# State-space scan and two MLP layers: the norm of a whole block of four units at once, state and outputs of a unit in one PSUM bank, first scores in other banks

## The chip, the cores and the metric

The kernel runs on one core of a Trainium2 chip. The metric is the time of one execution in device microseconds (us). A core has TensorE (PE: matmuls into PSUM; PEld are its weight loads), VectorE (DVE), ScalarE (ACT), GpSimd (POOL) and SyncE (SP, whose queue issues nearly all DMAs here). PSUM has eight banks of 512 fp32 columns on 128 partitions.

## What is computed

Three stages in a row, on 3072 tokens of 256 features. A state-space scan in chunks, over 4 batches and 8 heads:

```python
cum = np.cumsum(la, axis=-1)                      # la: log of the decays of a chunk
L = np.exp(cum[:, :, :, None] - cum[:, :, None, :]) * causal
CB = np.einsum('bhin,bhjn->bhij', Cc, Bc)
y_intra = np.einsum('bhij,bhjd->bhid', CB * L, xc)
y_inter = np.einsum('bhin,bhnd->bhid', Cc, state) * decay_to_i[:, :, :, None]
state = decay_full[:, :, None, None] * state + np.sum(Bx, axis=2)
```

Then a gated MLP behind a norm over the features, and a second MLP:

```python
rms = np.sqrt(np.mean(x * x, axis=-1, keepdims=True) + 1e-06)
xn = x / rms * rms_g
g = xn @ w_gate
x = (g / (1 + np.exp(-g))) * (xn @ w_val) @ w_out     # 256 -> 1536 -> 256
h = x @ w_in                                          # 256 -> 2048
out = (np.maximum(h, 0) + np.log1p(np.exp(-np.abs(h)))) @ w_out2
```

## The kernel before, in words

**Units and blocks.** The scan works on units: 128 tokens of one batch, all eight heads. There are 24, four batches by six; unit u is batch u % 4. Four units (one of each batch) make a block of 512 tokens, on which the MLP layers run; there are six blocks. Features lie on the partitions, two halves of 128 (`KD` = 2).

**One unit** (`unit`). DVE makes the products of decays by two scans of 128x512 (`ab`); the factors come from DRAM (`a_clip`) or, for the first four units, are copied across partitions by PE (`spread` of the decays, `p<-Sm,ident`). PE makes scores C·B into two PSUM tiles (`gps`); units 0 to 7 from tiles `hw`, later ones from `st` and `cz`. DVE multiplies each with the products (`decay`, 128x512). PE then runs the unit's groups: the outputs `yp` from state and chunk, and the new state's sum `sp`, in separate PSUM tiles. DVE updates the state `S` of the batch from `sp` (line 584; for the first four units ACT copies it); POOL builds the masked state `Sm` for the next unit of that batch.

**The norm of one unit** follows it (lines 589 to 621). ACT squares `yp` (`sq`, line 595); PE sums the squares over the features by matmuls with one column (`msum`, `a<-mean,sq`); DVE takes the inverse root in eight steps of 128x1 (`root`, lines 602 to 607: two to begin with, then three turns of two); PE spreads the root over the partitions (`a<-ident,rs`, one fp32 matmul of 128x128 that the trace shows as two passes); ACT scales `yp` by the gains (line 617); DVE multiplies (line 619), ACT copies the high part (`xxh`) and DVE subtracts for the low part (`xxl`, line 306). High and low parts are what the MLP's three-pass matmuls read.

**The MLP.** For each block, layer one has 12 steps `f` of twelve 128x512 matmuls (`front1`: `wg`, `wv`) and six (`back`: `wo`); layer two 16 steps of six (`front2`: `wi`) and six (`back`: `wp`). Between front and back stand an activation on ACT, a product on DVE in layer one, and the split into high and low part (`hw`, ACT line 299, DVE line 306). The order of stages is layer one of blocks 0 and 1, layer two of 0 and 1, then both layers of 2, 3, 4, 5. Units of later blocks run among the matmuls of the blocks before.

**Weights** come in 34 chunks of 512 KB through three buffers `wr`; ACT and DVE turn a chunk into high and low part. For the first four chunks PE makes the low part (`p<-wr,wil`). Forty matmuls with a constant (`filler`, `p<-mean`) stand in the first 44 us.

**Who sets the order.** A planner (`Plan`) writes it out. Every operation has an engine, an estimated length, a rank and the buffers that it reads and writes; `emit` runs through time with these estimates and takes at each point the operation that can start first, the lower rank ahead. What comes out is one fixed list per engine, in which each engine waits for its operands. The root's eight steps are estimated at 65 ns each. PSUM has three pools: `p` with four banks (fronts, decay spreads, fillers), `a` with two (scores, `yp`, `sp` and the norm's `nb` of units from block 1 on), `t` with two (the backs' sums, and `yp` in block 0). `SCORES_P` = 4 puts the scores of units 0 to 3 into `p`.

```python
DVE(0, rank[0], root, [nb, "mean"], [rs, ss], port=False, ns=8 * 65)
PE(220, rank[0], lambda: mm(nb()[:, 0:P], rs()[:, 0:1].to_broadcast([P, P]), ident, True, True), [rs, "ident"], [nb], 512)
```

Of the kernel before, what the change touches and what calls it, by code (L numbers as in the profile page):

```python
# [17 lines left out]
P = 128  # L18
# [8 lines left out]
NATIVE, SCORES_P, SPREAD = 8, 4, 4  # L27
# [14 lines left out]
XN_REST = ("dve",)  # L42
# [20 lines left out]
class Plan:  # L63
# [48 lines left out]
    def emit(self):  # L112
# [122 lines left out]
def tile_ssd_then_swiglu_then_softplus_mlp(  # L235
# [176 lines left out]
    xnT = {}  # L412

# [22 lines left out]
    def unit(u):  # L436
# [86 lines left out]
        gps = [pbuf("p" if u < SCORES_P else "a", [P, 4 * P]) for _ in range(2)]  # L523
# [28 lines left out]
        yp = pbuf("t" if blk_of[u] == 0 else "a", [P, KD, P])  # L552
# [34 lines left out]
        nxt()  # L587
        sq = buf("sq", [P, KD, P], F32, 2)
        ss, rs = buf("ss", [P, 1], F32, 2), buf("rs", [P, 2], F32, 2)
        nb = pbuf("a", [P, P + 1])  # L590

        def msum():
            for k in range(KD):
                mm(nb()[:, P:P + 1], sq()[:, k], mean, k == 0, k == KD - 1)
        ACT(256, rank[0], lambda: act.activation(out=sq(), in_=yp(), func=ACTF.Square), [yp], [sq])
        PE(400, rank[0], msum, [sq, "mean"], [nb], 8)

        def root():


            y, t = rs()[:, 0:1], rs()[:, 1:2]
            dve.tensor_scalar(out=ss(), in0=nb()[:, P:P + 1], scalar1=1e-6, scalar2=0.5, op0=ALU.add, op1=ALU.mult)  # L602
            dve.tensor_scalar(out=y.bitcast(I32), in0=ss().bitcast(I32), scalar1=-0.5, scalar2=float(0x5F3759DF - 2 ** 22 - 2 ** 31),  # L603
                              op0=ALU.mult, op1=ALU.add)
            for _ in range(3):
                dve.scalar_tensor_tensor(out=t, in0=y, scalar=y, in1=ss(), op0=ALU.mult, op1=ALU.mult)  # L606
                dve.scalar_tensor_tensor(out=y, in0=t, scalar=1.5, in1=y, op0=ALU.subtract, op1=ALU.mult)  # L607
        DVE(0, rank[0], root, [nb, "mean"], [rs, ss], port=False, ns=8 * 65)
        PE(220, rank[0], lambda: mm(nb()[:, 0:P], rs()[:, 0:1].to_broadcast([P, P]), ident, True, True), [rs, "ident"], [nb], 512)
# [41 lines left out]
    def front1(t, f, rank, new_table, early=False):  # L651
# [3 lines left out]
        xk = [(x, o) for x in (xh, xl) for o in range(bl["nu"])]  # L655
# [197 lines left out]
```

## Time and profile before

| | |
|---|---|
| median of 3 runs | 686.77 us (686.3 to 689.27) |
| the profiled execution | 689.41 us |
| its span (first to last instruction) | 686.9 us |
| PE busy | 668.5 us, 97% |
| DVE busy | 363.3 us, 53% |
| ACT busy | 311.6 us, 45% |
| POOL busy | 18.4 us, 3% |

The busy time of an engine is the time in which at least one of its instructions runs. The ends of matmuls are modelled, so that a matmul's listed length reaches into the next one. A wait is the idle time of an engine just before an instruction, put down to whatever released it last.

### The profile page before, as it was taken

The page shows a single profiled execution, that of the slowest core. Times are in us where ns is not written, and L with a number is a line of the kernel's source. Part 1 is how long each engine was busy: PE and PEld are TensorE (multiplying, and loading weights), DVE is VectorE, ACT ScalarE, POOL GpSimd, SP SyncE. Part 2 cuts the span into 40 slices and gives each one's busy share as a digit, 9 for nine tenths or more (in the row PEclk, how much of TensorE's full clock was granted, in tenths as well). Part 3 has the DMA queues.
Part 4 walks back from the last instruction along what each step waited for, and adds up shares of the span by engine and source line. Part 5 has one row for each costly group of instructions (what it writes and reads, how often), then busy time and mean ns, then how long its engine had stood idle before and what let it go on. Part 6 is the DMA issues. An engine that isn't in the chain of part 4 may idle for free.

```text
span 686.9 us, 9171 instructions
## 1 busy us (share of the span) xinstructions
PE 668.5 (97%) x3492; PEld 530.0 (77%) x3492; DVE 363.3 (53%) x722; ACT 311.6 (45%) x553; POOL 18.4 (3%) x28
## 2 busy tenths in 40 slices
PE   8899999999999999999999999999999999999997
PEld 6667778887778887778888777888777888887785
DVE  5989987787662226683433765432574322233222
ACT  4256746775444445232544332544423444422543
POOL 1000000001000000000000000000000000000000
PEclk9999999999999999999999999999999999999999
DMA  7546686657320004310231411050500000000000
GB/s 237 168 162 219 202 280 182 203 172 234 123 80 31 0 1 142 101 66 0 80 119 47 147 53 63 5 189 6 168 25 1 0 1 0 31 0 1 0 1 31
DMA packets 36778, 61.36 MB, mean 89 GB/s; under 512 B 3424, under 2 KB 18304, under 8 KB 36736
## 3 DMA queue, kind: packets, MB, share of 16 engines
q1 hardware_dynamic: 36304, 59.23, 26.8%
q10 hardware_dynamic: 432, 1.57, 0.7%
q8 instruction: 27, 0.44, 0.3%
q14 instruction: 15, 0.12, 0.1%
HBM read 47.58 MB, written 13.21 MB: 88 GB/s over the span
## 4 chain that ended last, share of the span: by engine, by line
PE 87%; DVE 8%; DMA 2%; issue 1%; SPq 1%; ACT 1%; DVEq 0%; ACTq 0%
PE p L268 48%; PE t L268 32%; PE a L268 7%; DVE rs L606 2%; DVE rs L607 2%; DMA xc<-in_xc 1%; DVE s L667 1%; DMA s<-in_ab 1%; DVE rs L603 1%; DVE ss L602 0%; DVE ab L500 0%; DVE hw L306 0%; ACT hw L299 0%; DVE xxl L500 0%; SPq L470 0%
## 5 line engine op out<-in xcount | busy, mean ns | idle before, releaser
L306 DVE TENSOR_TENSOR hw<-s,hw 128x512 fp32r<-128x512 f32 x162 | 111.8, 692 | 185.0 <-ACT hw L299 184.4
L299 ACT ACTIVATE hw<-s 128x512 fp32r<-128x512 f32 x162 | 101.8, 631 | 131.5 <-DVE s L667 103.6
L268 PE MATMUL t<-hw,wph 128*128 128x512 f32 x384 | 121.9, 398 | 0.2 <-DVE hw L306 0.2
L679 ACT ACTIVATE s<-p 128x512 f32<-128x512 f32 x96 | 57.0, 598 | 109.3 <-PE p L268 108.3
L667 DVE TENSOR_TENSOR s<-s,p 128x512 f32<-128x512 f32 x72 | 49.4, 686 | 75.1 <-PE p L268 68.1
L268 PEld LDWEIGHTS t<-hw,wph 128*128 128x128 f32 x384 | 71.2, 188 | 18.3 <-issue 1.0
L268 PE MATMUL t<-hw,woh 128*128 128x512 f32 x264 | 84.6, 401 | 0.3 <-DVE hw L306 0.2
L268 PE MATMUL p<-xxh,wih 128*128 128x512 f32 x192 | 76.3, 397 | 0.0
L268 PE MATMUL t<-hw,wpl 128*128 128x512 f32 x192 | 75.9, 396 | 0.0
L268 PE MATMUL p<-xxh,wil 128*128 128x512 f32 x192 | 75.9, 395 | 0.0
L268 PE MATMUL p<-xxl,wih 128*128 128x512 f32 x192 | 75.6, 394 | 0.2 <-DVE xxl L708 0.2
L663 ACT ACTIVATE s<-p 128x512 f32<-128x512 f32 x72 | 43.0, 598 | 45.3 <-PE p L268 42.8
L268 PE MATMUL p<-xxh,wgh 128*128 128x512 f32 x144 | 58.7, 408 | 0.0
L268 PE MATMUL p<-xxh,wvh 128*128 128x512 f32 x144 | 58.7, 408 | 0.0
L268 PEld LDWEIGHTS t<-hw,woh 128*128 128x128 f32 x264 | 48.1, 188 | 12.2 <-issue 0.8
L268 PE MATMUL p<-xxh,wgl 128*128 128x512 f32 x144 | 57.5, 399 | 0.0
L268 PE MATMUL p<-xxh,wvl 128*128 128x512 f32 x144 | 57.3, 398 | 0.0
L268 PE MATMUL p<-xxl,wgh 128*128 128x512 f32 x144 | 57.1, 396 | 0.0
L268 PE MATMUL p<-xxl,wvh 128*128 128x512 f32 x144 | 57.0, 396 | 0.0
L268 PE MATMUL t<-hw,wol 128*128 128x512 f32 x132 | 52.3, 396 | 0.0
L500 DVE TENSOR_TENSOR_SCAN ab<-ab,ident 128x512 f32<-128x512 f32 x40 | 48.4, 1217 | 0.0
L268 PEld LDWEIGHTS p<-xxl,wih 128*128 128x128 f32 x192 | 36.1, 188 | 9.2 <-DVE xxl L708 0.7
(113 smaller groups left out, 823.8 us busy)
## 6 DMA issues: line engine op xcount, KB each, us to landing
wr<-in_w SPq DMA_DIRECT2D x31, 512.0 KB, 3.3
ab<-a_clip SPq DMA_DIRECT2D x20, 512.0 KB, 4.0
parts<-wr SPq DMA_DIRECT2D x16, 512.0 KB, 3.7
xc<-in_xc SPq DMA_DIRECT2D x20, 256.0 KB, 4.1
st<-parts SPq DMA_DIRECT2D x16, 256.0 KB, 2.8
cz<-parts SPq DMA_DIRECT2D x32, 128.0 KB, 3.1
out_y<-s SPq DMA_DIRECT2D x12, 256.0 KB, 3.3
wr<-in_bc SPq DMA_DIRECT2D x8, 256.0 KB, 3.5
```

The source lines that it names most:

```text
L268: pe.matmul(out=o, lhsT=l, rhs=r, start=start, stop=stop, skip_group_check=True)
L299: ways = {"act": (act_ns(n), lambda: act.activation(out=out(), in_=in_(), func=ACTF.Copy)), "dve": (dve_ns(n, sbuf), lambda: dve.tensor_co ...
L306: return lambda: eng.tensor_tensor(out=out(), in0=in_(), in1=f32(hi()), op=ALU.subtract)
L500: DVE(512, rank[0], lambda t=t, d=d: dve.tensor_tensor_scan(out=t(), data0=d(), data1=ident4, initial=0.0, op0=ALU.mult, op1=ALU.add), dk ...
L603: dve.tensor_scalar(out=y.bitcast(I32), in0=ss().bitcast(I32), scalar1=-0.5, scalar2=float(0x5F3759DF - 2 ** 22 - 2 ** 31), op0=ALU.mult, ...
L606: dve.scalar_tensor_tensor(out=t, in0=y, scalar=y, in1=ss(), op0=ALU.mult, op1=ALU.mult)
L607: dve.scalar_tensor_tensor(out=y, in0=t, scalar=1.5, in1=y, op0=ALU.subtract, op1=ALU.mult)
L663: ACT(n, rank - EPI, lambda: act.activation(out=s()[:, 0:n], in_=ps[0]()[:, 0:n], func=ACTF.Silu), [ps[0]], [s, "table"] if new_table else ...
L667: DVE(n, rank - EPI, lambda: dve.tensor_tensor(out=s()[:, 0:n], in0=s()[:, 0:n], in1=ps[1]()[:, 0:n], op=ALU.mult), [s, ps[1]], [s], port= ...
L679: ACT(n, rank - EPI, lambda: act.activation(out=s()[:, 0:n], in_=hp()[:, 0:n], func=ACTF.Softplus), [hp], [s, "table"] if new_table and f ...
```

## The change

The norm leaves `unit` and becomes a function `norm` of several units: all four of a block at once, for block 0 of the first three and then of the fourth (`NORMS`). A unit now only squares and scales its outputs, into tiles of the whole block (`ysq`: squares under the tag `xxh`, scaled outputs under `xxl`, for which the xx pools' order is set by `rank`). When the last unit of a part is done, PE sums the squares of all its units one after the other, DVE takes the roots of up to four columns together, PE spreads them into one bank of up to 512 columns, and DVE multiplies, ACT copies and DVE subtracts over 384 or 512 columns at a time. For more than one unit the root has eleven steps, since the step with a scalar per partition becomes two plain multiplies. The planner's estimate for a step is 185 ns instead of 65.

`yp` and `sp` become two parts of one PSUM tile `ys` (256 and 64 columns). Only the first matmul into it clears the bank. All its readers name the one tile, so that the update of the state by DVE, the square and the scalings by ACT are kept from reading the bank at the same time. Scores of all units go into pool `a` (`SCORES_P` is gone), the sums and spreads of block 0 into pool `p`.

```diff
-NATIVE, SCORES_P, SPREAD = 8, 4, 4
+NATIVE, SPREAD = 8, 4
+NORMS = {0: [3, 1]}
...
-            l.sort(key=lambda b: (ops[b.ops[0]][1], b.ops[0]))
+            l.sort(key=lambda b: (ops[b.ops[0]][1] if b.rank is None else b.rank, b.ops[0]))
...
-        gps = [pbuf("p" if u < SCORES_P else "a", [P, 4 * P]) for _ in range(2)]
+        gps = [pbuf("a", [P, 4 * P]) for _ in range(2)]
...
-        yp = pbuf("t" if blk_of[u] == 0 else "a", [P, KD, P])
+        ys = pbuf("t" if blk_of[u] == 0 else "a", [P, KD * P + 2 * HD])
+        yp = lambda: ys()[:, 0:KD * P].rearrange("p (k i) -> p k i", k=KD)
+        sp = lambda: ys()[:, KD * P:KD * P + 2 * HD]
...
-        sp = None if last else pbuf("a", [P, 2 * HD])
...
-                    mm(sp()[32 * r:32 * r + 32], br()[:, 32 * r:32 * r + 32], xr()[:, 2 * HD * r:2 * HD * (r + 1)], True, True)
+                    mm(sp()[32 * r:32 * r + 32], br()[:, 32 * r:32 * r + 32], xr()[:, 2 * HD * r:2 * HD * (r + 1)], first, False)
...
-                    in1=sp(), op0=ALU.mult, op1=ALU.add), [S[b], sp, (xbt, "p")], [S[b]])
+                    in1=sp(), op0=ALU.mult, op1=ALU.add), [S[b], ys, (xbt, "p")], [S[b]])
...
+        ACT(256, rank[0], lambda: act.activation(out=sq()[:, :, c], in_=yp(), func=ACTF.Square), [ys], [(sq, o)])
+        for k in range(KD):
+            ACT(128, rank[0], lambda k=k: act.activation(out=y()[:, k, c], in_=yp()[:, k], func=ACTF.Copy, scale=g_sb[:, k:k + 1]),
+                [ys, "g"], [(y, k, o)])
+        for o0, n in parts_of(t):
+            if o == o0 + n - 1:
+                norm(t, o0, n, rank[0], step)
...
+    def norm(t, o0, nu, rank, step):
...
+        def msum():
+            for o in range(nu):
+                for k in range(KD):
+                    mm(nb()[:, o:o + 1], sq()[:, k, (o0 + o) * P:(o0 + o + 1) * P], mean, k == 0, k == KD - 1)
...
+            for _ in range(3):
+                if nu == 1:
+                    dve.scalar_tensor_tensor(out=q, in0=r, scalar=r, in1=m, op0=ALU.mult, op1=ALU.mult)
+                else:
+                    dve.tensor_tensor(out=q, in0=r, in1=r, op=ALU.mult)
+                    dve.tensor_tensor(out=q, in0=q, in1=m, op=ALU.mult)
+                dve.scalar_tensor_tensor(out=r, in0=q, scalar=1.5, in1=r, op0=ALU.subtract, op1=ALU.mult)
+        DVE(0, rank + step, root, [nb, "mean"], [rs, ss], port=False, ns=(8 if nu == 1 else 11) * 185)
+
+        def spread():
+            for o in range(nu):
+                mm(nb()[:, o * P:(o + 1) * P], rs()[:, 0, o:o + 1].to_broadcast([P, P]), ident, True, True)
```

**Where PE's list changes, in the stream.** PE around the norm of one unit of block 3, before (`a<-mean,sq` are the sums, `a<-ident,rs` the spread, the rest matmuls of layer one):

```order
L268 MATMUL a<-mean,sq 128x1 x2
L268 MATMUL t<-hw,woh 128x512 x2
L268 MATMUL t<-hw,wol 128x512
L268 MATMUL t<-hw,woh 128x512 x2
L268 MATMUL t<-hw,wol 128x512
L268 MATMUL a<-ident_68,rs 128x128
L268 MATMUL p<-xxh,wgh 128x512
```

and PE around the norm of the whole of block 3, after (the squares are now in a tile `xxh`):

```order
L268 MATMUL a<-mean,xxh 128x1 x8
L268 MATMUL p<-xxh,wvh 128x512
L268 MATMUL p<-xxl,wvh 128x512
L268 MATMUL p<-xxh,wvl 128x512
L268 MATMUL p<-xxh,wvh 128x512
L268 MATMUL p<-xxl,wvh 128x512
L268 MATMUL p<-xxh,wvl 128x512
L268 MATMUL p<-xxh,wgh 128x512
L268 MATMUL p<-xxl,wgh 128x512
L268 MATMUL p<-xxh,wgl 128x512
L268 MATMUL p<-xxh,wgh 128x512
L268 MATMUL p<-xxl,wgh 128x512
L268 MATMUL p<-xxh,wgl 128x512
L268 MATMUL a<-ident_68,rs 128x128 x4
```

Between sums and spread stand six matmuls of 128x512 before and twelve after, once in a block instead of four times.

**PE's list at the start.** Before (`p<-mean` are fillers, `p<-Sm,ident_68` spreads of decays, `p<-hw` scores of units 0 and 1, `t<-ab,xc` the outputs):

```order
L268 MATMUL p<-mean 128x512 x10
L268 MATMUL p<-Sm,ident_68 128x256 x4
L268 MATMUL p<-mean 128x512 x5
L268 MATMUL p<-hw 128x128 x8
L268 MATMUL p<-Sm,ident_68 128x256 x2
L268 MATMUL p<-mean 128x512 x2
L268 MATMUL p<-Sm,ident_68 128x256 x2
```

and after:

```order
L268 MATMUL p<-mean 128x512 x8
L268 MATMUL a<-hw 128x128 x8
L268 MATMUL p<-Sm,ident_68 128x256 x12
L268 MATMUL t<-xc 32x64 x4
L268 MATMUL t<-ab,xc 32x128 x8
L268 MATMUL a<-hw 128x128 x8
L268 MATMUL p<-Sm,ident_68 128x256 x4
L268 MATMUL p<-mean 128x512
```

The scores of unit 0 moved ahead of every spread.

**DVE's list at the start.** Before (`L500` are scans, `L547` decays, `L388` a weight step, `L753` and `L755` the running products, whose load is `s<-in_ab`):

```order
L388 SCALAR_TENSOR_TENSOR wr<-wr,zz_73 128x512
L500 SCALAR_TENSOR_TENSOR ab<-p,ident_68 128x512 x2
L520 TENSOR_TENSOR xc<-xc,ab 128x128
L388 SCALAR_TENSOR_TENSOR wr<-wr,zz_74 128x512
L547 TENSOR_TENSOR ab<-ab,p 128x512 x2
L500 SCALAR_TENSOR_TENSOR ab<-p,ident_68 128x512 x2
L388 SCALAR_TENSOR_TENSOR wr<-wr,zz_73 128x512
L520 TENSOR_TENSOR xc<-xc,ab 128x128
L753 TENSOR_SCALAR s<-s 96x256
```

and after (the same lines are L388, L502, L549, L791):

```order
L388 SCALAR_TENSOR_TENSOR wr<-wr,zz_73 128x512
L502 SCALAR_TENSOR_TENSOR ab<-p,ident_68 128x512
L388 SCALAR_TENSOR_TENSOR wr<-wr,zz_74 128x512
L502 SCALAR_TENSOR_TENSOR ab<-p,ident_68 128x512
L791 TENSOR_SCALAR s<-s 96x256
```

The running products moved ahead of two scans, two decays, two small products and a weight step.

## Rows read from the trace of the kernel before

**Rows 1.** The page, busy us (share of the span) and instructions of each engine.
```profile
PE 668.5 (97%) x3492; PEld 530.0 (77%) x3492; DVE 363.3 (53%) x722; ACT 311.6 (45%) x553; POOL 18.4 (3%) x28
```
**Rows 2.** PE's waits from 44 us on: who waited for whom, us, times, longest.
```profile
PE a L268 <- DVE rs L607: 7.0, 18, 0.6
PE t L268 <- DVE hw L306: 0.5, 2, 0.2
```
**Rows 3.** The chain that ended last: start us, us, what, near 113 us.
```profile
113.53 2.80 PE p L268 x12
```
**Rows 4.** Timeline at one norm: start us, us, engine, line, what, count [idle before].
```profile
159.10 0.72 PE L268 MATMUL t<-hw,woh 128*128 128x512 f32 x2
159.28 0.16 DVE L602 TENSOR_SCALAR ss<-a 128x1 f32<-128x1 f32 x1 [0.24 <-PE a L268]
...
160.36 0.39 PE L268 MATMUL t<-hw,wol 128*128 128x512 f32 x1
...
161.03 0.49 PE L268 MATMUL a<-ident,rs 128*128 128x128 f32 x2 [0.28 <-DVE rs L607]
...
161.27 0.47 PE L268 MATMUL p<-xxh,wvh 128*128 128x512 f32 x1
```
**Rows 5.** Stretches: length, busy us (count) by engine, granted clock, DMA share, GB/s.
```profile
20.00:23.50 3.50, 3.21 (x9) 2.67 (x10) 3.47 (x7) 0.42 (x1) 0.00 (x0) 0.51 1.00 263
23.50:44.00 20.50, 17.68 (x172) 12.78 (x171) 19.05 (x50) 9.15 (x23) 0.73 (x1) 1.00 0.41 143
44.00:47.40 3.40, 3.40 (x9) 2.62 (x9) 2.03 (x5) 1.50 (x3) 0.00 (x0) 0.50 0.48 151
47.40:110.00 62.60, 61.36 (x392) 48.02 (x392) 56.06 (x116) 36.98 (x69) 3.31 (x4) 1.00 0.73 237
```
**Rows 6.** Timeline of the first 44 us, DVE's steps and the first front matmul.
```profile
7.35 2.34 DVE L500 TENSOR_TENSOR_SCAN ab<-p,ident 128x512 f32<-128x512 f32 x2 [0.74 <-PE p L268]
...
10.86 1.28 DVE L547 TENSOR_TENSOR ab<-ab,p 128x512 f32<-128x512 f32 x2
...
16.99 0.29 DVE L753 TENSOR_SCALAR s<-s 96x256 f32<-96x256 f32 x1 [1.82 <-DMA s<-in_ab]
...
41.95 0.41 DVE L619 TENSOR_TENSOR sq<-sq,a 128x256 f32<-128x256 f32 x1
...
42.88 0.42 DVE L306 TENSOR_TENSOR xxl<-sq,xxh 128x256 fp32r<-128x256 f32 x1
...
43.50 0.50 PE L268 MATMUL p<-xxh,wgh 128*128 128x512 f32 x1
```
**Rows 7.** Groups of DVE instructions by form: busy us, mean ns, idle before.
```profile
L606 DVE SCALAR_TENSOR_TENSOR rs<-rs,ss 128x1 f32<-128x1 f32 x72 | 15.8, 220 | 2.6
L607 DVE SCALAR_TENSOR_TENSOR rs<-rs 128x1 f32<-128x1 f32 x72 | 12.0, 166 | 2.5
L619 DVE TENSOR_TENSOR sq<-sq,a 128x256 f32<-128x256 f32 x24 | 10.0, 418 | 4.7 <-PE a L268 4.6
...
L520 DVE TENSOR_TENSOR xc<-xc,ab 128x128 f32<-128x128 f32 x18 | 5.1, 285 | 0.4 <-DMA xc<-in_xc 0.4
```
**Rows 8.** Timeline of PE at the groups of unit 4.
```profile
47.95 0.61 PE L268 MATMUL a<-xc,Sm 128*128 128x128 f32 x4
48.49 0.32 PE L268 MATMUL a<-xc 128*32 128x64 f32 x8
...
49.18 1.17 PE L268 MATMUL p<-wr,wil 128*128 128x512 f32 x2
```
**Rows 9.** Timeline of ACT at the same norm as rows 4: square and scalings.
```profile
158.22 0.36 ACT L595 ACTIVATE sq<-a 128x256 f32<-128x256 f32 x1
...
158.48 0.62 ACT L617 ACTIVATE sq<-a,g_sb 128x128 f32<-128x128 f32 x2
```
**Rows 10.** Timeline: the unit's second decay on DVE and its groups on PE.
```profile
153.65 0.68 DVE L547 TENSOR_TENSOR ab<-ab,a 128x512 f32<-128x512 f32 x1
...
155.84 0.61 PE L268 MATMUL a<-xc,Sm 128*128 128x128 f32 x4
```
**Rows 11.** Loads of `hw` in the first 16 us, from issue to landing.
```profile
DMA to landing us min/median/max: 2.7/4.5/6.7
```
**Rows 12.** Timeline: SP issues the weight loads behind the first three.
```profile
33.46 11.59 SPq L379 DMA_DIRECT2D wr<-in_w  x4
```

More of the change, by code (lines that the diff above doesn't have):

```diff
@@ L412, in tile_ssd_then_swiglu_then_softplus_mlp @@
     xnT = {}
+    ysq = {}
+    xkeys = {}
     def base_of(u):
@@ L581, in unit @@
                 S[b] = buf("S", [P, 2 * HD], F32, NB)
-                COPY(64, rank[0], S[b], sp, [sp], [S[b]], False)
+                COPY(64, rank[0], S[b], sp, [ys], [S[b]], False)
             else:
                 DVE(64, rank[0], lambda: dve.scalar_tensor_tensor(out=S[b](), in0=S[b](), scalar=pr()[:, P - 1:P],
-                    in1=sp(), op0=ALU.mult, op1=ALU.add), [S[b], sp, (xbt, "p")], [S[b]])
[L587 to L609, printed above, removed]
+                    in1=sp(), op0=ALU.mult, op1=ALU.add), [S[b], ys, (xbt, "p")], [S[b]])
         nxt()
@@ new lines, in unit, with parts_of, root @@
+        for o0, n in parts_of(t):
+            if o == o0 + n - 1:
+                norm(t, o0, n, rank[0], step)
+    def parts_of(t):
+        o = 0
+        for n in NORMS.get(t, [blocks[t]["nu"]]):
+            yield o, n
+            o += n
+    def norm(t, o0, nu, rank, step):
+        c = slice(o0 * P, (o0 + nu) * P)
+        sq, y, r0 = ysq[t]
+        ss, rs = buf("ss", [P, 4], F32, 2), buf("rs", [P, 2, 4], F32, 2)
+        nb = pbuf("a" if t else "p", [P, 4 * P])
+        def msum():
+            for o in range(nu):
+                for k in range(KD):
+                    mm(nb()[:, o:o + 1], sq()[:, k, (o0 + o) * P:(o0 + o + 1) * P], mean, k == 0, k == KD - 1)
+        PE(230 * KD * nu, rank, msum, [(sq, o0 + o) for o in range(nu)] + ["mean"], [nb], 8)
+        def root():
+            r, q, m = rs()[:, 0, 0:nu], rs()[:, 1, 0:nu], ss()[:, 0:nu]
+            dve.tensor_scalar(out=m, in0=nb()[:, 0:nu], scalar1=1e-6, scalar2=0.5, op0=ALU.add, op1=ALU.mult)
+            dve.tensor_scalar(out=r.bitcast(I32), in0=m.bitcast(I32), scalar1=-0.5, scalar2=float(0x5F3759DF - 2 ** 22 - 2 ** 31),
+                              op0=ALU.mult, op1=ALU.add)
+            for _ in range(3):
[9 more added lines that the diff above has]
+                mm(nb()[:, o * P:(o + 1) * P], rs()[:, 0, o:o + 1].to_broadcast([P, P]), ident, True, True)
+        PE(240 * nu, rank + step, spread, [rs, "ident"], [nb], 512 * nu)
+        if not o0:
+            xnT[t] = [buf(f"xx{k}", [P, KD, 4 * P], F32R, 3) for k in "hl"]
+        h, l = xnT[t]
+        if t:
+            h.rank = l.rank = r0 + 0.01
+        for ks in ([slice(0, KD)] if nu < 4 else [slice(k, k + 1) for k in range(KD)]):
+            m = ks.stop - ks.start
+            n = m * nu * P
+            yk = [(y, k, o0 + o) for o in range(nu) for k in range(ks.start, ks.stop)]
+            hv, lv, yv = (lambda b=b, ks=ks: b()[:, ks, c] for b in (h, l, y))
+            DVE(n, rank + 2 * step, lambda yv=yv, m=m: dve.tensor_tensor(out=yv(), in0=yv(), in1=nb()[:, 0:nu * P].rearrange(
+                "p (o i) -> p o i", o=1).to_broadcast([P, m, nu * P]), op=ALU.mult), yk + [nb], yk, port=False)
+            COPY(n, rank + 2 * step, hv, yv, yk, [(h, o0, ks.start)])
+            REST(n, rank + 2 * step, lv, yv, hv, yk + [(h, o0, ks.start)], [(l, o0, ks.start)])
+            xkeys.setdefault(t, []).extend([(h, o0, ks.start), (l, o0, ks.start)])
@@ L654, in front1 @@
         xh, xl = xnT[t]
-        xk = [(x, o) for x in (xh, xl) for o in range(bl["nu"])]
+        xk = xkeys[t]
         ps = []
```

19 lines of the change are left out of this document (6 added, 13 removed).

## The prediction

> **What bounds the kernel now.** I read the busy shares first, then who waits for whom, then the timeline at one norm and in the first 44 us. TensorE (PE) is busy 97% of the span at the full clock; VectorE (DVE) 53%, ScalarE (ACT) 45% [rows 1]. So the end is set by PE's matmul count plus the places where PE stands still. From 44 us on, PE's idle time has one large cause: 7.0 us in 18 waits of a spread matmul for the last step of the inverse root; the next cause is 0.5 us [rows 2]. The true loss is larger than the listed idle time, because the profile lets a 128x512 matmul run 0.39 us while in a stream six of them take 1.40 us, 0.233 each [rows 3]: 0.16 us of each wait is hidden in the modelled tail. The timeline confirms it: the last stream matmul starts at 160.36, so the next could start at 160.59, and the spread starts at 161.03: 0.44 us lost, 0.28 of it listed [rows 4]. 7.0 + 18 x 0.16 = 9.9 us is what these waits cost in the stream.
>
> Ahead of the stream the bound is another: between 23.5 and 44 us DVE is busy 19.05 of 20.5 us [rows 5]. The first matmul of the first layer, at 43.50, follows the last subtraction of unit 3's norm on DVE, which ends at 43.30 [rows 6].
>
> **Part 1: one norm for a block instead of one per unit.** The twenty norms in the stream become five. What sets a wait: DVE takes up the sums 0.18 us after the first stream matmul behind them (159.28 against 159.10), its eight small steps and the hand-over to PE take 1.75 (159.28 to 161.03); PE has six matmuls, 1.40 us, to fill that [rows 4]. For four units the root has eleven steps: two to begin with, and three turns of multiply, multiply, subtract-and-multiply. The trace shows no multiply of 128x4; its nearest rows are the steps of 128x1, 166 and 220 ns long [rows 7], with a gap of some 0.035 to the next. The new root has six multiplies for three of the longer steps: 1.75 - 3 x 0.25 + 6 x (0.20 to 0.25) = 2.2 to 2.5 us, and the spread is ready 2.4 to 2.7 us after the sums. I take 2.4, nearer to the plain steps, since the longer one also reads an operand per partition. The new order puts twelve matmuls (2.8 us) there, eighteen in block 1. The wait is covered if DVE is free; one 128x512 operation in the way (0.6 us) leaves 0.2 to 0.5 us per block, 0 to 2.5 us in all. I take 0.5. Gain 9.4 us, bounds 7.4 to 9.9.
>
> The passes of PE stay the same in number: 96 for the sums, 48 for the spreads. In a row of their own they could be spaced more widely: a spread's two passes start 0.21 us apart and the next matmul follows 0.03 later [rows 4]; if every pass in the batch waited 0.21, three more such gaps in each of five blocks, 15 x 0.18 = 2.7 us, would be lost. The four passes from two different weights at unit 4, 0.54 us from start to the next matmul [rows 8], say 0.27 per pair against 0.24, so I take 0. DVE and ACT save work per block (four roots of 1.7 us become one of some 2.3), which earns nothing in the stream: DVE isn't the bound there [rows 1].
>
> **Part 2: state and outputs in one bank.** PE's work is the same. The state update on DVE and the square and two scalings on ACT now read one bank, and the built program lets them take turns: in nine of sixteen units DVE's update waits for both scalings, in the other seven the scalings or the square wait for the update. Before, they read two banks, and neither waited for the other. A turn holds DVE for the square and the scalings, 0.36 + 0.62 us [rows 9], so 1 us. Behind it on DVE stand scans, products and the decays of the next unit, for which PE waits. In the new order a unit's scores and its groups are nine to 24 matmuls apart, mostly twelve (2.8 us); the two decays need 0.6 us each, and in the trace one unit's second ended 1.5 us ahead of its groups (153.65 + 0.68 against 155.84) [rows 10]. Counting 0.5 us for scores, 0.2 for the hand-over and 1.3 for decays, twelve matmuls leave some 1.2 us; a turn of 1 us fits in. Price 0, bounds 0 and 16 x 1.0 = 16 us.
> Here a rule of the Trainium skill speaks against the change: PSUM — Partial Sum Buffer, section "PSUM bank collisions raise a hardware error", says that two engines may not touch one bank in the same 32-partition quadrant at once, whatever the columns, and that software must guard a bank by semaphores. No run here shows a collision; the turns above are that guard, and by it the two readers would never overlap, while by separate banks they might.
>
> **Part 3: the first 44 us.** Here the order changes most. (a) Unit 0's scores now stand ahead of all spreads of the decays (the matmuls that copy them across partitions for DVE's scans). Their loads, the third and fourth that SP issues, take 2.7 to 6.7 us in this stretch [rows 11], and PE waits for them with every spread behind it; the old order began the spreads first, so that DVE scanned from 7.35 on [rows 6]. (b) DVE meets the running products after two scans instead of four; their load ends a wait at 16.99 in both programs, as SP's issues ahead of it are the same. So at 17 us DVE has done two scans, two decays, two small products and a weight step less than before, and whatever (a) costs before that is hidden by this wait. From there, in starts to starts (two scans take 2.34, so the second starts 1.13 after the first; two decays 1.28, so 0.60 [rows 6]; each 0.08 less than its own length, which makes 0.20 of the 285 ns of a small product and 0.34 of the 418 of 128x256 [rows 7], and 0.87 for 128x768 by the same slope), the new list up to the last subtraction is: products 1.0, ten scans 11.3, ten decays 6.0, eight small products 1.6, one weight step 0.6, roots 2.2 + 1.6, multiply and subtract of three units 1.7, of the last 1.35 (41.95 to 43.30): 27.4 us. The old list: 1.0, eight scans 9.0, six decays 3.6, six small 1.2, one weight step 0.6, four roots 6.4, three multiplies and subtracts 2.0, the last 1.35: 25.2 us, so 42.2, and it ended at 43.30, with 1.1 us of waits. The new list ends at 44.4 with none. Its waits are more: the spread for three units stands behind fourteen fillers, and unit 4's scores behind unit 3's groups, each some 0.7 us of DVE waiting; if PE runs at 1.2 GHz, as it did from 20 to 23.5 us at a granted 0.51 [rows 5], each filler takes twice its 0.21 us (512 columns at 2.4 GHz), and the twelve ahead of unit 2's groups cost up to 2.6 us. I put the end at 47.3: start of the stream 4.0 us later (bounds 1.1 to 5.5; with all 26 fillers slow, 9.6).
> Two things come back. Unit 4's groups, 47.95 to 49.18 in the stream [rows 8], now run ahead of it: 1.2 us. And the stream lost 3.4 us x 0.5 = 1.7 us to the half clock between 44 and 47.4 [rows 5], after DVE had kept PE waiting for unit 3's root; the new order has the weights' remainders, unit 4's groups and four fillers there. I take half, 0.8. Net 4.0 - 1.2 - 0.8 = +2.0 us, bounds -1.8 to +8.4.
> (c) The first three weight remainders move from 32 to 37 us to behind unit 3's sums, near 44, and with them the next weight loads, which SP issued from 33.46 on as their buffers came free [rows 12]. A load lands after 3.3 us, four conversions take 2.5: ready near 50. Their matmuls come after 36 others, 8.4 us into the stream, past 55. Price 0; if that cover went, some 5 us.
>
> **Sum.** The profiled execution took 689.41 us, of which 686.9 is span; minus 9.4, plus 2.0, gives 682.0. The median of the three timed runs is 686.77, 2.6 lower; the same difference of 7.4 from it gives 679.4, and I forecast **679**.
>
> **Rivals.** (1) The head eats the gain: PE stays at half clock through both runs of fillers, which then cost 2.6 and 3.0 us more, and DVE waits for them. Net head +2.0 + 5.6, result 686.8 - 9.4 + 7.6 = 685. For it: a granted 0.51 at 20 us after PE had waited; against: the fillers themselves are work. (2) The turns decide: slower. If DVE comes to a unit's decays more than the spare 1.2 us late, every further turn is paid by PE. With 16 units at 1 us, on top of the head: 686.8 - 9.4 + 2.0 + 16 = 695; the point from which the kernel gets slower is some 0.5 us lost per unit. For it: units now follow each other every twelve to twenty matmuls, while DVE's own work for a unit (two scans, two decays, small ones) is 4 us; against: DVE was 90% busy from 47 to 110 us [rows 5] and PE hardly waited for it there [rows 2]. (3) All of the gain: the root covered in every block, the head's lateness of some 2 us paid back by unit 4's groups and the clock: 686.8 - 9.9 - 1.0 = 676. (4) The change doesn't do what it says: the root is still not covered as DVE takes it up late; 2.5 us stay, 681, inside the forecast's range.
>
> **Chances.** Forecast with (4), 677 to 683.3: 0.60; (1) 0.17; (2) 0.09; (3) 0.14. A measurement of this kernel tells some 0.5%, 3.4 us, from no change. Faster by more: 0.58 + 0.14 = 0.72; within: 0.19; slower: 0.09. The range goes from the lower half of (3) to the upper end of (1): 675 to 686.5.
>
> **What would show it.** Waits of the spread for the root: from 7.0 us to under 1 us in the stream. First matmul of the first layer near 47.5 instead of 43.5; DVE idle for some 3 us before 17 us. Waits of PE for the decays or for the weights' remainder after 48 us: none over 0.5 us in sum; several us would be rival 2 or lost cover in (c). A granted clock near 0.5 while fillers run would be rival 1. I am wrong if the stream (first matmul of layer one to the end) isn't shorter by 8 to 11 us.

## The result, and the profile after

The changed kernel takes **677.31 us** (median of 4 runs, 677.17 to 679.11), the kernel before 686.53 on the same chip (684.85 to 689.27): ratio 0.9868, interval 0.9831 to 0.9904. The interval excludes 1: the kernel is faster, by 1.3%. That is 1.7 us below the forecast of 679, inside the range, and about as near to the 676 of rival 3.

The page of the changed kernel, against [rows 1]:

```profile
span 675.5 us, 9002 instructions
...
PE 665.6 (99%) x3492; PEld 533.5 (79%) x3492; DVE 343.9 (51%) x580; ACT 308.4 (46%) x541; POOL 20.6 (3%) x28
```

PE's waits from 48 us to the end, against [rows 2] (engine, tile and line, what it waited for: us, times, longest):

```profile
PE t L268 <- DVE hw L306: 0.4, 2, 0.2
PE p L268 <- DVE xxl L746: 0.2, 1, 0.2
```

The 7.0 us in 18 waits for the root are gone. The timeline of PE and DVE at the norm of one block (start and length in us, engine, line, operation, tiles, count; against [rows 4]):

```profile
187.87 1.84 PE L268 MATMUL a<-mean,xxh 128*128 128x1 f32 x16
...
189.57 0.71 PE L268 MATMUL t<-hw,wph 128*128 128x512 f32 x2
189.74 0.16 DVE L628 TENSOR_SCALAR ss<-a 128x4 f32<-128x4 f32 x1 [1.57 <-PE a L268]
...
191.72 0.16 DVE L637 SCALAR_TENSOR_TENSOR rs<-rs 128x4 f32<-128x4 f32 x1
...
191.79 2.33 DVE L502 TENSOR_TENSOR_SCAN ab<-ab,ident 128x512 f32<-128x512 f32 x2
...
192.22 0.40 PE L268 MATMUL p<-xxh,wil 128*128 128x512 f32 x1
...
192.45 1.05 PE L268 MATMUL a<-ident,rs 128*128 128x128 f32 x8
...
193.26 0.48 PE L268 MATMUL p<-xxh,wih 128*128 128x512 f32 x1
```

The sums begin at 187.87, DVE takes them up at 189.74, 0.17 us behind the first matmul after them, and its eleven steps end 2.14 us later (191.72 + 0.16). PE works on twelve matmuls meanwhile, of which the last starts at 192.22, and begins the spread 0.23 behind it: nothing lost.

The first stretch (all ahead of the first matmul of layer one), DVE's waits (in brackets: idle time before, and what ended it):

```profile
12.89 1.22 DVE L502 TENSOR_TENSOR_SCAN ab<-p,ident 128x512 f32<-128x512 f32 x1 [6.47 <-PE p L268]
...
28.02 1.23 DVE L502 TENSOR_TENSOR_SCAN ab<-ab,ident 128x512 f32<-128x512 f32 x1 [0.81 <-DMA ab<-a_clip]
...
39.02 0.95 DVE L656 TENSOR_TENSOR xxl<-xxl,p 128x768 f32<-128x768 f32 x1 [1.02 <-PE p L268]
40.72 0.69 DVE L549 TENSOR_TENSOR ab<-ab,a 128x512 f32<-128x512 f32 x1 [0.74 <-PE a L268]
...
45.28 0.42 DVE L656 TENSOR_TENSOR xxl<-xxl,p 128x256 f32<-128x256 f32 x1 [0.80 <-PE p L268]
46.18 0.62 DVE L306 TENSOR_TENSOR xxl<-xxl,xxh 128x256 fp32r<-128x256 f32 x1 [0.48 <-ACT xxh L299]
```

and PE's rows there:

```profile
7.47 0.79 PE L268 MATMUL a<-hw 16*128 16x128 f32 x2 [2.77 <-DMA hw<-in_bc]
8.78 2.07 PE L268 MATMUL a<-hw 16*128 16x128 f32 x14 [0.52 <-DMA hw<-in_bc]
10.78 8.64 PE L268 MATMUL p<-Sm,ident 96*128 96x256 f32 x24
...
33.28 4.97 PE L268 MATMUL p<-mean 128*128 128x512 f32 x14
38.09 0.83 PE L268 MATMUL p<-ident,rs 128*128 128x128 f32 x6
...
47.21 0.40 PE L268 MATMUL p<-xxh,wgh 128*128 128x512 f32 x1
```

PE waits for the loads of unit 0's scores with every spread behind it, so that DVE's first scan stands at 12.89 instead of 7.35 [rows 6]. The loads are not all of it: behind the wait the scores and spreads run at half speed, passes of the spreads 0.43 us apart up to 17.3 us and 0.22 from there on. e11 (below), whose list begins the same way, shows the granted clock of that stretch, which fell while PE waited for the loads (from and to, length, busy us and count by engine, granted clock, DMA):

```profile
7.61:17.85 10.24, 9.73 (x33) 7.83 (x33) 4.79 (x8) 1.96 (x3) 0.00 (x0) 0.50 0.63 173
```

By the distances of the same matmuls in e5, where they run at full speed, some 1.9 us of DVE's 6.47 are the half clock (an estimate). The first matmul of layer one comes at 47.21 instead of 43.50. From there to the end it is 628.3 us (675.5 - 47.21), before 643.4 (686.9 - 43.50).

**Where the 15.1 us of the stream went**, by adding up the distances from each matmul's start to the next one's in both traces: 9.9 are the waits for the root; 2.6 a loss of its own kind (below: the second 128x512 matmul behind a run of small ones starts 0.31 to 0.34 instead of 0.23 us after the first; 63 such places before, 33 after); 1.6 matmuls at half clock ahead of 47.4; 1.2 unit 4's groups, now ahead of the stream; 1.0 waits ahead of the sums. Against it the sums and spreads themselves cost 0.5 us more (sums 1.1 more, spreads 0.6 less), and smaller differences 0.7. Against 15.1 stands the start, 3.7 later: 11.4 in the two profiled executions. The profile of before is of an execution 2.6 us above its median (689.41 against 686.77), that of after is at its median (677.4), so that the medians show 9.2.

### The profile page after: what moved, and what is told of

Read it like the earlier page. It is cut to its first block, busy times and chain, and to the rows that moved or that the text cites. A ratio compares the mean times of both kernels' runs of the same rounds, so it can differ in the third digit from the quotient of the medians.

```text
span 675.5 us, 9002 instructions
## 1 busy us (share of the span) xinstructions
PE 665.6 (99%) x3492; PEld 533.5 (79%) x3492; DVE 343.9 (51%) x580; ACT 308.4 (46%) x541; POOL 20.6 (3%) x28
## 4 chain that ended last, share of the span: by engine, by line
PE 95%; DMA 2%; DVE 1%; issue 1%; ACT 0%; SPq 0%; DVEq 0%
PE p L268 52%; PE t L268 35%; PE a L268 7%; DMA ab<-a_clip 1%; DMA hw<-in_bc 1%; DVE ab L502 0%; DVE hw L306 0%; ACT hw L299 0%; DVE ab L549 0%; DVE xxh L549 0%; DVE s L793 0%; DVE xxl L746 0%; DVE s L705 0%; DVE wr L388 0%; ACT s L717 0%
## 5 line engine op out<-in xcount | busy, mean ns | idle before, releaser
L306 DVE TENSOR_TENSOR hw<-s,hw 128x512 fp32r<-128x512 f32 x162 | 113.4, 702 | 187.3 <-ACT hw L299 186.8
L268 PE MATMUL p<-xxh,wvh 128*128 128x512 f32 x144 | 57.1, 397 | 0.0
L502 DVE TENSOR_TENSOR_SCAN ab<-ab,ident 128x512 f32<-128x512 f32 x40 | 50.3, 1277 | 5.1 <-DMA ab<-a_clip 4.9
```

The costliest lines, as they stand in the source:

```text
L268: pe.matmul(out=o, lhsT=l, rhs=r, start=start, stop=stop, skip_group_check=True)
L306: return lambda: eng.tensor_tensor(out=out(), in0=in_(), in1=f32(hi()), op=ALU.subtract)
L502: DVE(512, rank[0], lambda t=t, d=d: dve.tensor_tensor_scan(out=t(), data0=d(), data1=ident4, initial=0.0, op0=ALU.mult, op1=ALU.add), dk ...
```

## Experiments

The theory ahead of them: the gain is the cover of the root; the loss is the later start; the rest nearly nothing. Its rivals: the batching as such makes the gain; turns at the shared bank cost or give something. All runs, with the start of layer one (its first matmul), the rest of the span behind it, and DVE's busy and idle time from 6 us to that start. Behind the start lie the groups of 20 units in before, e1 and e10, of 18 in e6, of 19 in the others (1.2 us each).

The ratios are to runs of the kernel before taken beside each (medians 686.53 to 687.50).

| kernel | median, us | ratio to before, interval | start | rest of span | DVE busy + idle |
|---|---|---|---|---|---|
| before | 686.53 | | 43.50 | 643.4 | 32.9 + 4.7 |
| after | 677.31 | 0.9831 to 0.9904 | 47.21 | 628.3 | 29.9 + 11.3 |
| e1 before, estimate 185 | 676.70 | 0.9820 to 0.9872 | 43.15 | 631.7 | 34.6 + 2.6 |
| e2 after, estimate 65 | 682.09 | 0.9907 to 0.9953 | 45.65 | 634.0 | 29.8 + 9.8 |
| e3 after, norm per unit from block 1 on | 676.47 | 0.9813 to 0.9863 | 46.68 | 627.8 | 29.9 + 10.7 |
| e4 after, two banks | 677.64 | 0.9835 to 0.9887 | 47.09 | 627.9 | 31.9 + 9.2 |
| e5 after, first scores in p | **670.67** | 0.9728 to 0.9783 | 39.72 | 628.4 | 29.7 + 4.0 |
| e6 e5, block 0 per unit | 676.57 | 0.9809 to 0.9863 | 48.38 | 625.8 | 35.3 + 7.1 |
| e7 e6, 56 fillers | 672.36 | 0.9756 to 0.9805 | 43.26 | 627.1 | 34.4 + 2.9 |
| e8 e7, all norms per unit | 675.09 | 0.9786 to 0.9836 | 43.65 | 629.4 | 34.1 + 3.6 |
| e9 after, spreads ahead of scores | 671.03 | 0.9747 to 0.9794 | 41.34 | 628.4 | 28.4 + 6.9 |
| e10 e1, 56 fillers | 678.19 | 0.9845 to 0.9891 | 41.97 | 632.4 | 33.3 + 2.7 |
| e11 after, block 0 per unit | 687.02 | 0.9972 to 1.0009 | 54.77 | 628.7 | 32.8 + 16.0 |
| e12 e5, block 0 all four at once | 673.45 | 0.9778 to 0.9838 | 41.14 | 631.0 | 28.0 + 7.1 |

**e1: the estimate alone**, in the kernel before.

```diff
-        DVE(0, rank[0], root, [nb, "mean"], [rs, ss], port=False, ns=8 * 65)
+        DVE(0, rank[0], root, [nb, "mean"], [rs, ss], port=False, ns=8 * 185)
```

> The kernel before, with one number changed: the planner's estimate for a step of the inverse root, 185 ns instead of 65. Norm per unit, two banks and scores in their old places all stay. In the new order nearly every norm of the stream has twelve 128x512 matmuls (2.8 us) between its sums and its spread, where it had six. Theory (the gain comes from the cover of the root, and a cover can be had without batching): waits of the spread for the root in the stream fall from 7.0 us to under 0.7, time 686.5 - 9.9 = 676.6, and with some 1 us either way in the first 44 us, 675.5 to 678. Rival (batching is needed, since twenty single roots get in DVE's way or are taken up late): 3 us or more of waits stay, 681 or more.

PE's waits from 44 us to the end:

```profile
PE t L268 <- DVE hw L306: 0.5, 2, 0.2
PE p L268 <- DVE xxl L708: 0.2, 1, 0.2
PE a L268 <- DVE sq L619: 0.2, 1, 0.2
```

No wait for the root stays in the stream. **One number does as much as the whole change** (676.70 against 677.31, intervals that overlap).

**e2: the batch with the old estimate.**

```diff
-        DVE(0, rank + step, root, [nb, "mean"], [rs, ss], port=False, ns=(8 if nu == 1 else 11) * 185)
+        DVE(0, rank + step, root, [nb, "mean"], [rs, ss], port=False, ns=(8 if nu == 1 else 11) * 65)
```

> The changed kernel with the planner's estimate for a step of the root back at 65 ns. The norm stays batched, but only six matmuls (1.40 us) stand between sums and spread of blocks 2 to 5, and twelve in block 1. Theory: the eleven steps take 2.1 us, with take-up and hand-over 2.4 to 2.5, so 1.0 to 1.1 us is lost in each of four blocks, some 0.85 of it listed as waits for the root: 677.3 + 4.2 = 681.5, 680.5 to 682.5. Rival (batching alone covers the root, or DVE's lighter load does): under 1 us of waits, 677 to 678.

PE and DVE at the norm of block 2, and then at that of block 1:

```profile
189.06 0.71 PE L268 MATMUL t<-hw,wph 128*128 128x512 f32 x2
189.24 0.16 DVE L628 TENSOR_SCALAR ss<-a 128x4 f32<-128x4 f32 x1 [1.57 <-PE a L268]
...
190.31 0.40 PE L268 MATMUL t<-hw,wpl 128*128 128x512 f32 x1
...
191.21 0.16 DVE L637 SCALAR_TENSOR_TENSOR rs<-rs 128x4 f32<-128x4 f32 x1
...
191.43 1.16 PE L268 MATMUL a<-ident,rs 128*128 128x128 f32 x8 [0.72 <-DVE rs L637]
```

```profile
90.02 0.71 PE L268 MATMUL t<-hw,woh 128*128 128x512 f32 x2
...
90.96 0.69 DVE L388 SCALAR_TENSOR_TENSOR wr<-wr,zz 128x512 int32<-128x512 int32 x1
...
91.57 0.15 DVE L628 TENSOR_SCALAR ss<-a 128x4 f32<-128x4 f32 x1
...
93.54 0.16 DVE L637 SCALAR_TENSOR_TENSOR rs<-rs 128x4 f32<-128x4 f32 x1
...
93.75 1.16 PE L268 MATMUL a<-ident,rs 128*128 128x128 f32 x8 [0.69 <-DVE rs L637]
```

With six matmuls the spread starts 1.12 us after the last of them (191.43 - 190.31) instead of 0.23: 0.89 lost in each of four blocks. From the end of the sums to the spread it is 2.37 us (189.06 to 191.43). The fifth wait is another: in block 1 there were twelve matmuls, but DVE was at weight steps and took up the sums only at 91.57, 1.55 us behind the first matmul after them instead of 0.18, so that twelve did not do. (The changed kernel has eighteen there.) 4.4 us are lost to the root, and the median rises by 4.8. Against the kernel before 5.4 us of gain remain, with five waits for the root where eighteen stood.

**e3: the norm per unit again from block 1 on**, with the estimate of 185.

```diff
-NORMS = {0: [3, 1]}
+NORMS = {0: [3, 1], **{t: [1, 1, 1, 1] for t in range(1, 6)}}
```

> The changed kernel with the norm per unit again from block 1 on; block 0 stays at three and one, and estimate, one bank and pools stay. Twelve matmuls or more stand between sums and spread in nearly all of the twenty norms. Theory: the root stays covered (waits under 0.7 us), and what is lost is the price of interrupting the stream: thirty more runs of small matmuls, of which each makes the second 128x512 behind it start 0.08 us late, 2.4 us, less some 0.5 us as sums are cheaper in pairs than in eights: 677.3 + 1.9 = 679.2, 678 to 680.5. Rival (the batching itself made the gain): waits come back, 683 or more. Second rival (interruptions cost nothing): 677.

PE at one of the norms:

```profile
260.30 0.50 PE L268 MATMUL a<-mean,xxh 128*128 128x1 f32 x4
260.66 0.48 PE L268 MATMUL p<-xxh,wgh 128*128 128x512 f32 x1
260.98 0.39 PE L268 MATMUL p<-xxl,wgh 128*128 128x512 f32 x1
...
263.55 0.38 PE L268 MATMUL a<-ident,rs 128*128 128x128 f32 x2
263.69 0.48 PE L268 MATMUL p<-xxh,wgh 128*128 128x512 f32 x1
264.00 0.39 PE L268 MATMUL p<-xxl,wgh 128*128 128x512 f32 x1
```

The interruption is there (260.66 to 260.98 and 263.69 to 264.00 are 0.31 instead of 0.23), thirty more of them. But the time is 2.7 us under the theory's 679.2, near the second rival's 677: the theory missed that short rows of passes are cheaper. Four passes of sums take 0.36 us (260.30 to 260.66), a spread's two 0.14 (263.55 to 263.69). Per unit that is 0.36 + 0.08 + 0.14 + 0.08 = 0.66 us, 2.64 for four; the batch takes 1.70 (187.87 to 189.57) + 0.08 + 0.81 (192.45 to 193.26) + 0.08 = 2.67. Within a row the passes stand 0.11 us apart in both; each row has a single step of 0.03, whatever its length, so many short rows have more of these. So the batch is worth nothing to PE in the stream: 627.8 against 628.3.

**e4: two banks again** for outputs and state.

```diff
-        ys = pbuf("t" if blk_of[u] == 0 else "a", [P, KD * P + 2 * HD])
-        yp = lambda: ys()[:, 0:KD * P].rearrange("p (k i) -> p k i", k=KD)
-        sp = lambda: ys()[:, KD * P:KD * P + 2 * HD]
+        yp = pbuf("t" if blk_of[u] == 0 else "a", [P, KD, P])
+        sp = None if last else pbuf("a", [P, 2 * HD])
...
```

> The changed kernel with outputs and state of a unit in two PSUM tiles again, as before, so that DVE's state update and ACT's square and scalings need not take turns; all else stays. Theory (turns are paid by idle time of DVE and ACT): the stream from the first matmul of layer one to the end keeps its 628 us within 1; the first 47 us change by up to 2 either way as the planner places units 0 to 3 anew: 677.3, 675.5 to 679.5. Rival (turns cost PE time): stream shorter by 2 us or more. Other rival (one bank pays because it leaves a buffer of the pool free): stream longer by 2 us or more, with waits of PE for decays or scores.

677.64, start and rest within 0.4 us of the changed kernel. (The plan here also puts one more unit's scores, 1.1 us, ahead of the start, so the price is known to about 1 us.) The turns, in the changed kernel from 48 us on:

```profile
DVE S L588 <- ACT xxh L597: 4.2, 3, 2.1
...
ACT xxl L599 <- DVE S L588: 1.3, 3, 0.4
...
DVE S L588 <- ACT xxl L599: 0.6, 2, 0.3
```

DVE waits 4.8 us in five turns, ACT 1.3 in three, and PE for none of it.

**e5: the first scores back in pool p.**

```diff
-        gps = [pbuf("a", [P, 4 * P]) for _ in range(2)]
+        gps = [pbuf("p" if u < 4 else "a", [P, 4 * P]) for _ in range(2)]
```

> The changed kernel with the scores of units 0 to 3 in pool p again, as before; norms, estimate and one bank stay. PE then begins four spreads of the decays ahead of unit 0's scores, so DVE scans from 7 us on instead of 12.9. Theory (the later start of the stream, 47.21 against 43.50, comes from the 6.5 us that DVE stands idle before 12.9): the first matmul of layer one at 44 to 45.5, the stream as in the changed kernel, so 674.2 to 676, say 675. Rival (the idle time of DVE is hidden by its later waits for PE: 1.02, 0.74, 0.80 and 0.48 us near the end of the head, behind fillers and groups): start not before 46.5, time 677.

PE's first spreads and DVE's first scans, and DVE's share of the time to the start in one row (from and to, length, busy time, granted clock, DMA share, GB/s):

```profile
6.17 1.99 PE L268 MATMUL p<-Sm,ident 96*128 96x256 f32 x8 [0.61 <-DVE Sm L770]
...
7.33 2.34 DVE L502 TENSOR_TENSOR_SCAN ab<-p,ident 128x512 f32<-128x512 f32 x2 [0.53 <-PE p L268]
...
12.24 2.33 DVE L502 TENSOR_TENSOR_SCAN ab<-p,ident 128x512 f32<-128x512 f32 x2
```

```profile
6.00:39.72 33.72, 29.73 (x58) 0.95 0.68 197
```

and the same row of the changed kernel:

```profile
6.00:47.21 41.21, 29.88 (x60) 0.96 0.58 162
```

The same 29.8 us of work, 7.3 us less of standing still, 5.9 of it ahead of the first scan (0.53 instead of 6.47): the start comes 7.5 us earlier, the rest is unchanged, and the median falls by 6.6, more than the theory gave. **This version beats both kernels.**

**e9: is it the pool or the order?** The scores stay in `a`, and unit 0's only wait for its first scan.

```diff
-            PE(1100, rank[0], scores, [(bct, b % 2, 0), (bct, b % 2, 1)], list(gps), 512)
+            PE(1100, rank[0], scores, [(bct, b % 2, 0), (bct, b % 2, 1)] + [(abt, 0)] * (u < 1), list(gps), 512)
```

> The changed kernel with its scores in pool a, but unit 0's scores wait for the first scan of unit 0, so that PE makes six spreads of the decays before them; nothing else is changed by hand. Theory (what the moved scores cost is their place ahead of the spreads: DVE idle before the stream 11.3 us in the changed kernel, 4.0 in e5_after_scores_in_p, with the same 30 us of work): DVE's first scan near 7.3, its idle time before the stream down to 4 to 6 us, start of the stream at 40 to 42, time 670.5 to 672.5. Rival (the pool itself costs: scores in a hold up units' groups or each other): start not before 45, 675.5 to 677.5.

671.03: it is the order. The idle time fell to 6.9 us, not to 4 to 6; the start is in the expected place, 1.6 us behind e5's.

**e6, e7: block 0 per unit on top of e5, with 40 and with 56 fillers.**

```diff
-NORMS = {0: [3, 1]}
+NORMS = {0: [1,1,1,1]}
...
-FILL, FILL0 = 40, 8
+FILL, FILL0 = 56, 8
```

> As e5_after_scores_in_p, and the norm of block 0 per unit, so that the whole first stretch is made as before, while blocks 1 to 5 keep the norm of a block. Theory (the order of the scores is what counts, and the batch of three in block 0 holds the first layer back by its long multiply and subtraction, 0.95 us each on DVE, and a wait of 1.02): start at 43.5 to 45, time 673.5 to 675.5. Rival (batching in block 0 is neutral): the same as e5 within 0.7 us.

> As e6_after_scores_in_p_norm0_per_unit, with 56 fillers in place of 40; the planner puts 13 of the new ones between unit 3's sums and its spread, 2 behind that and one after. Theory (the half clock of 3.4 to 10.2 us that the kernel before and e1 had at the start of the stream came behind a stretch in which PE stood idle, and each slow 128x512 matmul costs 0.2 us; fillers there keep the clock): full clock at the start of the stream, 1 to 2 us less than e6, less any delay by fillers that run late. Rival (fillers only delay unit 4's groups and the spread for unit 3): 0 to 2 us more than e6.

Both expectations for e6 missed: it is 5.9 us slower than e5. e7's had the sign and not the size: 4.2 us less than e6, where 1 to 2 were expected. The same stretch in e6 and then in e7 (from and to, length, busy us and count by engine, granted clock, DMA):

```profile
32.78:43.02 10.24, 8.44 (x64) 5.49 (x64) 7.97 (x27) 2.92 (x9) 1.23 (x1) 0.50 0.18 54
```

```profile
32.78:43.02 10.24, 9.88 (x94) 6.41 (x93) 9.82 (x27) 3.83 (x11) 0.73 (x1) 1.00 0.40 119
```

In e6 PE ran this stretch at a granted 0.50, which began while it stood 2.8 us for a root (31.8 to 34.6); with sixteen more fillers it ran at 1.00 and did 94 matmuls in it instead of 64. DVE waits 1.3 us for unit 3's sums and 1.3 for its spread in e6, and for neither in e7. The start moved from 48.38 to 43.26, of which 1.2 is unit 5's groups, which only e6 has ahead of it; the rest is the clock together with a new order (nine matmuls for the weights' low parts between those sums and that spread in e6, six in e7), which were not separated. Between e5 and e7, both with little idle time of DVE, the batch of three shows best: DVE has 29.7 instead of 34.4 us to do before the stream, and the stream starts 3.5 us earlier, although e7 has sixteen fillers more.

**e11: block 0 per unit, scores ahead of the spreads** as in the changed kernel.

```diff
-NORMS = {0: [3, 1]}
+NORMS = {0: [1, 1, 1, 1]}
```

> The changed kernel with the norm of block 0 per unit; scores stay in pool a and ahead of the spreads. Theory (in the first stretch the batch of three saves DVE some 4 us of work: 29.9 us busy between 6 us and the stream's start against 34.4 in e7, and the scores' place costs idle time by itself): start of the stream 2 to 4 us later than 47.21, time 679 to 681. Rival (the batch costs as much by its wait of 1.02 us and its long operations as it saves): 676.5 to 678.

687.02: all of the gain is gone, far outside both expectations. PE and DVE near the end of its first stretch:

```profile
43.11 0.80 PE L268 MATMUL p<-ident,rs 128*128 128x128 f32 x2 [3.65 <-DVE rs L637]
...
47.08 1.01 PE L268 MATMUL p<-mean,xxh 128*128 128x1 f32 x4
...
53.33 0.38 PE L268 MATMUL p<-ident,rs 128*128 128x128 f32 x2
...
54.77 0.50 PE L268 MATMUL p<-xxh,wgh 128*128 128x512 f32 x1
```

```profile
53.81 0.42 DVE L656 TENSOR_TENSOR xxl<-xxl,p 128x256 f32<-128x256 f32 x1 [3.40 <-PE p L268]
```

Only 2.9 us of the 7.6 by which it starts later are DVE's work (32.8 against 29.9); 4.7 are idle. PE waited 3.65 us for unit 2's root and ran at half clock from 41.74, within that wait, to 51.98, and nine matmuls for the weights' low parts between unit 3's sums and its spread kept DVE waiting for 3.40. How these three share the 4.7 was not separated.

**e8: the norm per unit in every block, on top of e7.**

```diff
-NORMS = {0: [1,1,1,1]}
+NORMS = {t: [1, 1, 1, 1] for t in range(6)}
```

> As e7_e6_56_fillers, with the norm per unit in all blocks, estimate 185 ns. Theory (batching is worth nothing in the stream: the passes of sums and spreads are dearer in a row, 106 against 92 ns for a sum, 101 against 70 for a spread's pass, and thirty fewer interruptions of 0.08 us pay just that): within 1 us of e7. Rival (in e3_after_norm_per_unit the 0.8 us that it was faster were real, from sums and spreads): 0.5 to 1 us faster than e7.

Slower by 2.7 us, which neither side had. Most of what differs stands at the start of the stream: PE waits 0.8 us for a subtraction of the norm, and one unit's scores, 1.1 us, now lie behind the start. Another 0.6 us of wait stands at 263 us, where a unit's multiply came late behind a scan of DVE that had waited 2.1 us for its load. So the plan around the start differs by some 2 us for reasons of its own, and e3, with the first stretch nearly unchanged, is the cleaner test.

**e10: more fillers in e1.**

```diff
-FILL, FILL0 = 40, 8
+FILL, FILL0 = 56, 8
```

> The kernel before with only the estimate at 185 ns (as e1_before_est185) and 56 fillers in place of 40. Theory (e1 lost some 2.1 us of its stream and part of its first 43 us to 10.24 us at half clock, which began behind PE's waits for unit 2's root, 3.1 us; fillers there keep the clock): no half clock before the end, 673.0 to 675.5. Rival (no gain, as fillers delay units' groups): 676 to 679.

Nothing was gained: 678.19. In the profiled execution the granted clock was 1.0, as the theory said; it is the fastest of the five (676.83), and the other four have 0.995 to 0.998 (e1: 0.991 to 0.992 in all four). In the profiled executions of the two the start came 1.2 us earlier and the rest is 0.8 longer, with waits that e1 lacks (0.4 us for a square by ACT, 0.6 for a product's low part): 674.4 against 674.8. Why the medians stand 1.5 the other way stays open.

**e12: block 0 all at once, on top of e5.**

```diff
-NORMS = {0: [3, 1]}
+NORMS = {0: [4]}
```

> As e5_after_scores_in_p, with the norm of block 0 of all four units at once. Theory (a root of 2.1 us replaces 2.1 and 1.75, but nothing of the norm can begin before unit 3's groups, so that sums, root, spread, multiplies, copies and subtractions stand in a row between those and the stream): start 1 to 2.5 us later than 39.72, 671 to 673.5. Rival (DVE's saving decides): 0.5 to 1.5 us faster than e5, 669 to 670.

673.45, as the theory said: start 1.4 us later, and two more waits of PE behind it, 1.2 us for a subtraction and 0.9 for a decay. Three and one is the better cut, by 2.8 us of the medians.

## Why the prediction was right, point by point

**The root: right, with its numbers.** The forecast had the spread ready 2.4 us after the sums; e2 shows 2.37. It had steps of 0.20 to 0.25 us; all eleven stand 0.19 to 0.205 apart, 128x4 as 128x1. The loss of 9.9 us, of which 2.9 lay hidden in modelled tails, came back whole: the distances added up give 9.9. The 0.5 us that I kept for DVE being late came to 0, since the block where DVE is late has eighteen matmuls; with twelve it would be 0.85 (e2).

**What made that gain: the forecast left it with the batch, and it is the estimate.** The working counted the matmuls that now stand behind the sums, which is right, but told it under the heading of one norm for a block. e1 has the gain without the batch, e2 the batch with half of the gain lost. What the batch itself does is make fewer waits of an uncovered root; once it is covered, e3 shows nothing left to earn.

**Passes: the price of 0 was wrong in both parts and right in sum.** The 0.21 us that I read between a spread's two passes was itself an effect of the wait: that spread takes 0.24 us (161.03 to 161.27 [rows 4]), one without a wait 0.14 (263.55 to 263.69 in e3). So ending the waits gave back another 1.9 us, which stood in no term. In a row passes stand 0.11 apart, and the bound of 2.7 us is 1.3 for the spreads; the sums, for which I had no price, add 1.3 (e3 against the changed kernel). Thirty fewer interruptions of 0.085 us, which I had not counted at all, pay these back. By my own mark, a stream shorter by 8 to 11 us, this part was wrong: it is 15.1, of which 1.2 for unit 4's groups and 1.6 for the clock stood in the sum elsewhere (the clock at 0.8), and 2.6 for interruptions and 1.0 for waits ahead of the sums stood nowhere.

**One bank: price 0, shown to about 1 us** (e4). The turns fall into idle time of DVE and ACT. The Trainium skill (PSUM — Partial Sum Buffer, section "PSUM bank collisions raise a hardware error") asks for just such turns where two engines read one bank; the trace shows them as the waits above, and here they cost PE nothing. Rival 2 is out.

**The first stretch: the sum right by luck, the pieces not told apart.** Forecast: start 47.3 + 0.2, measured 47.21. The list from the products to the last subtraction was 27.4 us by my count; it is 46.80 - 15.75 - 3.85 of waits = 27.2. The products came at 15.75, not 16.99: their load landed earlier, so the wait that was to hide the late scans wasn't there, and DVE's idle time was 6.5 us up to 12.9, where I had some 3 before 17. The waits behind the products were 3.85 instead of 2.9. These errors, 1.2 us early and 1.0 late, nearly cancel. And +4.0 was two large effects of opposite sign: the scores ahead of the spreads cost 7.5 us of start (e5; 5.9 by e9), the batch of three gave back some 3.5 (e5 against e7), in this order 7.6 (e11). In my lists the scores' step is 5.1 us of scans, decays and small products moved behind 17 us, and the batch saves 2.9 of roots, multiplies and subtractions. The half clock left the stream wholly (I took half). It fell instead on the scores and spreads ahead of 17 us, which the working had nowhere, and from 34.34 to 37.75 (granted 0.50) on the fillers at 33.28 to 38.09, 0.34 us each, with DVE waiting 1.02 us behind them: rival 1's mechanism, at a fraction of its price. Rival 3 named the right cover and the wrong head. The weights' cover held: no wait of PE for them.

**The total.** The working took 7.4 us off; between the executions that were profiled it is 11.4, and only the medians, 9.2 apart, bring the time to within 1.7 us of 679. That the number is so near is in part luck.

## What to carry to other kernels

Where a planner orders the work, compare its estimates with the trace first: steps estimated at 65 ns that stand 190 to 250 apart cost 10 us here, and correcting that one number gave what a rewrite of the norm gave. A batch earns where the engine that it relieves is the limit (DVE ahead of the stream), or where it makes fewer waits (e2); with DVE off the limit and the waits covered it earned nothing (e3). When a part's net effect is small, ask which of its edits pull apart: one line of this change, undone, is worth another 6.6 us.

## What the runs showed of the hardware

- A run of sums, of a spread's passes or of a unit's groups costs PE, beside its own time, 0.08 to 0.11 us at the second 128x512 matmul behind it, the first starting on time (e3: 263.55, 263.69, 264.00). Behind the scores of 128x256 it is not there: sixteen runs in the kernel before, the second matmul 0.23 us after the first.
- Passes of sums and spreads stand 0.11 us apart, with one step of 0.03 in each row. So a pass costs more on average in a long row: 0.09 us for four sums, 0.106 for sixteen; 0.07 for two spread passes, 0.10 for eight. Right behind a wait of PE the second pass of a spread came 0.21 us after the first (kernel before).
- DVE's steps on 128x1, 128x3 and 128x4 all stand 0.19 to 0.205 us apart, a step with a scalar per partition 0.25.
- A stretch at half clock (32.78 to 43.02) stands with a start some 4 us later in e6, where DVE waited for PE's sums and spread in it; one as long in e9 (26.80 to 37.04) left the start within 1.6 us of e5's, and e10's profiled execution, without one, is 0.4 us shorter than e1's with one. That its price hangs on whether somebody waits for PE there is my reading; no run has the clock alone changed.
